# Folding an attention memory into gate weights: split float32 passes, or plain float32 tiles of 64 rows by 32 columns

## The chip, the cores and the metric

The kernel runs on one core of one Trainium2 chip. The metric is the device time of one execution in microseconds (us). Engines are called by the names of the profile: PE is TensorE's matmuls and PEld its weight loads, DVE is VectorE, ACT is ScalarE, POOL is GpSimd, SP is SyncE, which issues most DMAs.

## The reference

Attention to a memory of 32 slots for each of 8 heads and 4 batches, then a gated layer and a second layer for 2304 tokens (the softmax sums carry + 1e-9, left out here):

```python
a = softmax(phi, axis=2)                      # over the 576 tokens
k_m = einsum('bhsm,bhsd->bhmd', a, k)         # 32 x 64 for each head
v_m = einsum('bhsm,bhsd->bhmd', a, v)
attn = softmax(q @ k_m.T / 8) @ v_m           # 4 x 8 x 576 x 64
x = attn, tokens by 512
x = ((x @ w_a) * (x @ w_b)) @ w_o1            # 512 -> 1536 -> 512
h = x @ w_in                                  # 512 -> 2048
out = (h * sigmoid(1.702 h)) @ w_out          # 2048 -> 512
```

## The kernel before

The attention's last product is never made. Since `x @ w_a` is `P @ (v_m @ w_a)` with P the softmax weights of a batch (576 tokens by 8 heads x 32 slots), the kernel **folds** the memory into the weights: for each batch and each of six groups `g` of 256 hidden columns it makes `eff = v_m @ [w_a | w_b]`, 256 rows (in two chunks `c` of 4 heads) by 512 columns. `gated` multiplies P with eff, `proj` with w_o1.

PE multiplies float32 exactly enough in two ways. One is a plain float32 matmul, which the trace shows as two records. The other splits both operands into a high and a low part that fit a shorter format (`hi_lo`: ACT writes the high part, DVE or POOL subtracts it) and makes three ordinary passes, high x high, low x high, high x low (`PASSES`). Nearly all matmuls of the kernel are of the second kind.

The folds before:

- Group 0 (`fold0`, L756) runs in the attention phase, batch by batch, in plain float32. `bdv[b]` holds the memory of a batch as the stationary operand: 128 partitions are 2 heads of 64, and for each pair `r` of heads 64 columns are the 2 x 32 slots, zero where head and slot don't belong together. Two matmuls of 128 rows by 64 columns fill a bank.
- Groups 1 to 5 (`fold`, L787) run behind the attention for two batches `2 pb` and `2 pb + 1` together. `split_memory` has split bdv into `vhl`; `decode_piece` and `split_weights` have decoded each piece of w_a and w_b (128 rows, 256 columns of both) from the 64-bit input and split it too. For each pair of heads three passes of 128 x 128 with 512 values streamed fill one bank: the upper 64 partitions belong to one batch, the lower to the other. Most folds are in two halves of two pairs each, at different places of `main`.
- `fold_out` (L802, L804) takes a bank away: ACT writes the high part of eff, DVE the low one, before in two instructions each of 64 partitions.

Buffers: eight PSUM banks; `dm_s`, three to six temporary buffers in which inputs are decoded; `wab_s`, four places for split weights of the fold, inside the tile `wv`, which the trace names in L787. `close_attention` makes the tiles of the second phase when the attention is over.

The order on each engine is set when the program is built. Streams of steps (generators) ask for an engine, a time and a duration; `Order.run` keeps a clock for each engine and takes the step that can start first. On the chip each engine works through its list in that order and waits by semaphores for its operands. `Lengths.three` is the planner's guess for three passes. `main` is the stream that sets PE's order behind the attention.

Of the kernel before, what the change touches and what calls it, by code (L numbers as in the profile page):

```python
# [8 lines left out]
F32 = mybir.dt.float32  # L9
# [17 lines left out]
MBN = 8  # L27
HOLDD = {4: ("attn", 1, 0), 6: ("attn", 3, 0)}
# [6 lines left out]
PW0 = 4  # L35
PW = 5.5
# [138 lines left out]
def tile_mem_attention_moe_moe2(  # L175
# [195 lines left out]
    slots_of = {"wab": wab_s, "o1": whl_s}  # L371
    decoded = {}

    def decode(first, last, prio):
        if first in HOLDD:
            yield ("mark", *HOLDD[first])
        for i in range(first, last):
            name, part, _, n = pieces[i]
            t = yield "mark", "raw", i
            m = yield "slot", dm_s  # L380
# [23 lines left out]
    def decode_piece(t, i, name, part, n, m):  # L404
# [31 lines left out]
        if plain:  # L436
            dm_s.release(m, t)
            od.mark(t, *name, part)
        elif name[0] == "in":
# [14 lines left out]
        else:  # L454
# [4 lines left out]
            yield from split_weights(t, name, part, wt[name][0], m, dst, n)  # L459

    def w_ab_view(tile_):
        return tile_.rearrange("p (i r f) -> p i r f", i=2, r=1)
# [4 lines left out]
    def split_weights(t, name, part, whole, m, src, n):  # L467
        view = {"o1": w_out_view, "wab": w_ab_view}[name[0]](whole)
        r = slice(part * n, (part + 1) * n)
        t = yield from hi_lo(t, view[:, HI, r, :], view[:, LO, r, :], src, 512)  # L470
        dm_s.release(m, t)
        od.mark(t, *name, part)
# [8 lines left out]
    def row(b, h):  # L481

        return (h + 2 * (b % 2)) % HG * M
# [200 lines left out]
    def close_attention():  # L684
# [4 lines left out]
        for c in range(NHG):  # L689
            yield "mark", "eff", 0, B - 1, c, 0  # L690
# [6 lines left out]
        nonlocal py, pz  # L697
        py = tc.alloc_tile_pool(name="py", bufs=1, side="right", reuse_waits="tile")
        pz = tc.alloc_tile_pool(name="pz", bufs=1, side="right", reuse_waits="tile")
        n = 4 * CW  # L700
        big["y0"] = y0 = py.tile([P, 7 * 4 * N2 + 8], F32R, name="y0")
        nw = 2 * NHG * n
        big["wv"] = wv = pz.tile([P, nw + B // 2 * 2 * 2 * NHG * P], F32R, name="wv")
        wab_m, vhl_m = wv[:, :nw], wv[:, nw:]
# [3 lines left out]
        give(wab_s, [wab_m[:, i * n:(i + 1) * n] for i in range(2 * NHG)])  # L708
# [7 lines left out]
        for i in (HI, LO):  # L716
# [3 lines left out]
        vhl.extend(x.rearrange("p (i r m) -> p i r m", i=2, r=2 * NHG) for x in (  # L720
            vhl_m[:, i * 4 * NHG * P:(i + 1) * 4 * NHG * P] for i in range(B // 2)
        ))
        od.spawn(8, split_memory())


    py, pz, vhl, g1_t, g1_all, eff_y, big = None, None, [], {}, [], [], {}
# [21 lines left out]
    def fold0(b):  # L748
        for c in range(NHG):
# [4 lines left out]
            for r in range(2):  # L754
                o = row(b, 2 * r)
                nc.tensor.matmul(  # L756
                    ps[0][o:o + D, :], bdv[b][:, 2 * c + r, :], wt["wab", 0, 2 * c + r][0], start=True, stop=True
                )
            od.spawn(0, fold_out(t, 0, b, c, 0, slice(0, P), ps, [1]))

    def split_memory():

        for b in range(B):
            t = 0.0
            for c in range(NHG):
                t = max(t, (yield "mark", "bdv", b * NHG + c))
            for e in range(2):
                o = (e + b) % 2 * 2 * M
                dst = vhl[b // 2].rearrange("p i (c e) m -> p i c e m", e=2)[:, :, :, e, o:o + 2 * M]
                src = bdv[b].rearrange("p (c e) m -> p c e m", e=2)[:, :, e, :]  # L770
                t1 = yield from hi_lo(t, dst[:, HI], dst[:, LO], src, 2 * D)
                od.mark(t1, "vhl", b, e)
        more = [[bdv_m[:, i * 512:(i + 1) * 512], t1] for i in range(2)]
# [3 lines left out]
    def fold(g, pb, pairs=range(2 * NHG)):  # L777
        t0 = 0.0
        for b in (2 * pb, 2 * pb + 1):
            for e in range(2):  # L780
                t0 = max(t0, (yield "mark", "vhl", b, e))
        for r in pairs:
            t = max(t0, (yield "mark", "wab", g, r, 0))
            t, ps = yield PE, t, Lengths.three, bank_m
            w = w_ab_view(wt["wab", g, r][0])
            for n, (sw, mv) in enumerate(PASSES):
                nc.tensor.matmul(  # L787
                    ps[0], vhl[pb][:, sw, r, :], w[:, mv, 0, :], start=(n == 0), stop=(n == len(PASSES) - 1)
                )
            if pb == B // 2 - 1:  # L790
                wab_s.release(wt["wab", g, r], t)
            left = [2]
            for i in range(2):
                half = (i + r) % 2
                od.spawn(
                    i, fold_out(t, g, 2 * pb + i, r // 2, half, slice(half * D, (half + 1) * D), ps, left)
                )

    def fold_out(t, g, b, c, part, half, ps, left):
        hi, lo = (eff_of(g, b)[c][half, i, :] for i in (HI, LO))  # L800
        t, _ = yield ACT, t, act(512, True)
        nc.scalar.activation(out=hi, in_=ps[0][half, :], func=AF.Copy)  # L802
        t, _ = yield DVE, t, dve(512)
        nc.vector.tensor_tensor(out=lo, in0=ps[0][half, :], in1=f32(hi), op=ALU.subtract)  # L804
        left[0] -= 1
        if left[0] == 0:
            bank_m.release(ps, t)
        od.mark(t, "eff", g, b, c, part)

    def gated(g, b, u):  # L810
        t0 = 0.0
        for c in range(NHG):
            t0 = max(t0, (yield "mark", "attn", b * NHG + c, u))
            for i in range(2 if g else 1):
                t0 = max(t0, (yield "mark", "eff", g, b, c, i))
# [146 lines left out]
    def room_early():  # L962

        crowded()
        rest = views(big["y0"], YN, 9, 14 * WN)
# [142 lines left out]
    def combine_weights(g):  # L1108
        m = [decoded[("in", g), k] for k in range(2)]
        t = yield "mark", "decoded", ("in", g), 0  # L1110
        t = max(t, (yield "mark", "decoded", ("in", g), 1))
        s = yield "slot", win_s
# [321 lines left out]
    def main():  # L1434
# [14 lines left out]
        yield from fold(1, 1, range(NHG))  # L1449
# [140 lines left out]
```

## Time and profile before

| what | value |
|---|---|
| time, median of 3 runs | 782.17 us (781.64 to 783.31) |
| the profiled execution's own time | 783.01 us |
| its span | 781.2 us |
| PE busy | 768.4 us, 98% |
| DVE, ACT, POOL busy | 82%, 53%, 47% |
| chain that ended last | PE 92%, of it the gate L831 18%, the fold L787 3% |

The span is the time from the first to the last instruction of the program. The chain that ended last is followed back from the last instruction; shares of PE on it are read as what the end depends on. A matmul's record starts when PE takes it and its end is modelled, so a step's cost to PE is the distance of starts. Times on ACT, DVE and POOL matter where PE waits for them. In the groups by line, "64x512 fp32r" is what one instruction writes; a weight load or matmul has its rows and columns in the array ahead of that, as 128*64.

### The profile page before, as it was taken

Reading aid. Unit: us, or ns where it says so; the run is one execution under the profiler, and the core shown is the slowest. Engines: PE = TensorE matmul, PEld = TensorE weight load, DVE = VectorE, ACT = ScalarE, POOL = GpSimd, SP = SyncE. Lnnn points to the kernel's source line nnn. Section 1 sums busy time; section 2 is a strip of 40 time slices with the busy share of each in tenths; the row PEclk is TensorE's granted clock in tenths of the full one; section 3 lists DMA queues with packets and bytes.
Section 4 is the critical chain, followed back from the end, with each engine's and each line's share of the span. In section 5 each row is a group of like instructions: output and inputs, shape, how many; then the busy total and the mean of one; then the engine's idle time right before and its main releaser. Section 6 shows DMA issues by size and latency. Waiting matters only on the chain.

```text
span 781.2 us, 14295 instructions
## 1 busy us (share of the span) xinstructions
PE 768.4 (98%) x5216; PEld 708.7 (91%) x5216; DVE 638.7 (82%) x1132; ACT 416.9 (53%) x924; POOL 369.6 (47%) x347
## 2 busy tenths in 40 slices
PE   8999999999999999999999999999999999999997
PEld 7777789999989899899999999999998878889997
DVE  4878988999999987886989777777796786857886
ACT  4567768664655645544755555544563445534442
POOL 1223215554645544535799666333261036763563
PEclk9999999999999999999999999999999999999999
DMA  8856510122222312130013635544678855934421
GB/s 283 331 176 200 159 29 28 55 81 81 71 65 85 105 56 81 55 98 11 1 29 97 209 130 185 176 156 156 201 254 288 273 170 186 292 88 135 137 81 29
DMA packets 70183, 103.96 MB, mean 133 GB/s; under 512 B 5856, under 2 KB 48864, under 8 KB 70112
## 3 DMA queue, kind: packets, MB, share of 16 engines
q1 hardware_dynamic: 64656, 93.64, 37.7%
q10 hardware_dynamic: 5456, 9.41, 3.4%
q8 instruction: 41, 0.67, 0.4%
q14 instruction: 30, 0.25, 0.1%
HBM read 75.24 MB, written 27.79 MB: 132 GB/s over the span
## 4 chain that ended last, share of the span: by engine, by line
PE 92%; DVE 3%; DMA 2%; ACT 1%; issue 1%; POOL 1%; SPq 0%; ACTq 0%; DVEq 0%; POOLq 0%
PE bank L1135 22%; PE bank L831 18%; PE bank L1336 14%; PE bank L1367 10%; PE bank L864 10%; PE bank L887 10%; PE bank L787 3%; DMA phi<-in_phi_dram 1%; PE bank L619 1%; PE bank L575 1%; DMA kv<-in_v_dram 1%; PE bank L756 1%; PE bank L494 1%; ACT et L547 0%; DVE mx L541 0%
## 5 line engine op out<-in xcount | busy, mean ns | idle before, releaser
L1177 DVE TENSOR_TENSOR acc<-bank,acc 128x384 f32<-128x384 f32 x168 | 89.7, 553 | 31.6 <-PE bank L1135 19.5
L302 DVE TENSOR_TENSOR attn<-acc,attn 128x512 fp32r<-128x512 f32 (+2 forms) x94 | 90.7, 987 | 25.0 <-ACT attn L308 25.0
L302 POOL TENSOR_TENSOR acc<-acc 128x512 f32<-128x512 f32 (+2 forms) x63 | 81.0, 1299 | 46.1 <-DVE attn L302 24.2
L308 ACT ACTIVATE attn<-acc 128x512 fp32r<-128x512 f32 (+2 forms) x114 | 66.4, 602 | 55.0 <-PE bank L1367 18.0
L1187 ACT ACTIVATE acc<-acc 128x384 f32<-128x384 f32 x96 | 49.3, 523 | 52.7 <-DVE acc L1177 51.7
L844 ACT ACTIVATE gr<-bank 128x288 f32<-128x288 f32 x96 | 38.8, 404 | 65.2 <-PE bank L831 63.7
L302 POOL TENSOR_TENSOR y<-gr,y 128x288 fp32r<-128x288 f32 x40 | 36.3, 908 | 50.3 <-ACT y L308 50.2
L847 DVE TENSOR_TENSOR gr<-bank,gr 128x288 f32<-128x288 f32 x96 | 43.0, 450 | 14.4 <-PE bank L831 8.5
L831 PE MATMUL bank<-attn,eff 128*128 128x288 f32 x384 | 54.3, 296 | 0.0
L831 PEld LDWEIGHTS bank<-attn,eff 128*128 128x128 f32 x384 | 52.1, 188 | 1.3 <-issue 0.9
L864 PE MATMUL bank<-g,whl_b 128*128 128x288 f32 x384 | 52.8, 295 | 0.1
L1135 PE MATMUL bank<-attn,y 128*128 128x384 f32 x288 | 52.3, 335 | 0.0
L864 PEld LDWEIGHTS bank<-g,whl_b 128*128 128x128 f32 x384 | 51.7, 188 | 0.6 <-POOL whl_b L302 0.3
L887 PE MATMUL bank<-y,whl_a 128*128 128x512 f32 (+1 forms) x240 | 51.5, 370 | 0.0
L1135 PEld LDWEIGHTS bank<-attn,y 128*128 128x128 f32 x288 | 50.1, 188 | 0.0
L419 POOL TENSOR_SCALAR dm<-dm 128x512 f32<-128x512 f32 x21 | 34.6, 1651 | 32.1 <-ACT dm L417 32.1
L302 POOL TENSOR_TENSOR y<-acc,y 128x256 fp32r<-128x256 f32 (+1 forms) x22 | 20.1, 924 | 61.7 <-ACT y L308 61.7
L887 PEld LDWEIGHTS bank<-y,whl_a 128*128 128x128 f32 x240 | 41.9, 188 | 8.0
L302 POOL TENSOR_TENSOR g<-gr,g 128x288 fp32r<-128x288 f32 x28 | 27.0, 967 | 40.8 <-ACT g L308 40.6
L907 DVE TENSOR_TENSOR acc<-bank,acc 128x512 f32<-128x512 f32 (+1 forms) x72 | 38.4, 552 | 5.9 <-PE bank L887 5.2
L1336 PE MATMUL bank<-wv,attn 128*128 128x512 f32 x180 | 43.0, 393 | 0.0
L417 ACT ACTIVATE dm<-raw 128x512 f32<-128x512 f32 x41 | 27.0, 667 | 28.3 <-DMA raw<-in_moe_w_b_dram 12.3
(269 smaller groups left out, 2024.4 us busy)
## 6 DMA issues: line engine op xcount, KB each, us to landing
g2d<-acc SPq DMA_DIRECT2D x96, 192.0 KB, 2.3
raw<-in_moe_w_out_dram SPq DMA_DIRECT2D x28, 512.0 KB, 4.5
acc<-g2d SPq DMA_DIRECT2D x10, 1024.0 KB, 6.0
raw<-in_moe_w_in_dram SPq DMA_DIRECT2D x16, 512.0 KB, 3.8
acc<-g2d SPq DMA_DIRECT2D x16, 512.0 KB, 5.8
raw<-in_moe_w_a_dram SPq DMA_DIRECT2D x20, 256.0 KB, 2.7
raw<-in_moe_w_b_dram SPq DMA_DIRECT2D x20, 256.0 KB, 3.0
q<-in_q_dram SPq DMA_DIRECT2D x8, 576.0 KB, 6.3
```

The costliest lines, as they stand in the source:

```text
L302: (nc.gpsimd if e == POOL else nc.vector).tensor_tensor(out=dst, in0=in0, in1=in1, op=op)
L308: nc.scalar.activation(out=hi, in_=src, func=AF.Copy)
L831: nc.tensor.matmul(ps[0][:, :U], e[c][:, sw, i * CW + j * P:i * CW + (j + 1) * P], attn(b, mv, c, u * U, U), start=(n == 0), stop=(n == 3 ...
L844: nc.scalar.activation(out=gr[0], in_=pa_[0][:, :U], func=AF.Copy)
L847: nc.vector.tensor_tensor(out=gr[0], in0=pb[0][:, :U], in1=gr[0], op=ALU.mult)
L864: nc.tensor.matmul(ps[0][:, :U], w[:, sw, j, mb * P:(mb + 1) * P], g1[0][:, j, mv, :], start=(n == 0), stop=(n == 3 * G1 - 1),)
L887: nc.tensor.matmul(ps[0][:, :e - o], w[:, sw, j, mb * P:(mb + 1) * P], g1_all[mv][:, j, o:e], start=(n == 0), stop=(n == 3 * G1 - 1),)
L1135: nc.tensor.matmul(ps[0][:, :N2], w[:, sw, r, :], y[mv][r], start=(n == 0), stop=(n == 5))
L1177: nc.vector.tensor_tensor(out=s[0], in0=ps[0][:, :N2], in1=x[0], op=ALU.add)
L1187: nc.scalar.activation(out=c[0], in_=c[0], func=AF.Gelu_apprx_sigmoid)
L1336: nc.tensor.matmul(ps[i, s][0], b[0][:, sw, c - o, :], wo2[c][:, mv], start=(c == n == 0), stop=(c == 4 * K4 - 1 and n == 2),)
L1367: nc.tensor.matmul(ps[name][0][:, :NB], x[0][:, sw, c, :], moving(b, h // 2 + c, mv), start=(h == c == n == 0), stop=(h > 0 and c == K4 - ...
```

## The change

The fold of groups 1 to 5 uses plain float32 and no split operands. For a pair of batches it is made in one piece: 16 matmuls, each of 64 rows (one head's 64 values) by 32 columns (its 32 slots), with 512 values streamed, into four banks (one for each batch `i` and chunk `c`). `z` is the half of the 64-row tiles: 0 the upper partitions, 1 the lower. Eight matmuls, of both halves, four column places and two batches, stand one behind the other and use different parts of the array; the upper and the lower ones write different banks. The second eight fill what is missing.

With that the memory isn't split but copied (`bdw`, in the tile `plain`), the weights stay where they were decoded (ten buffers of `plain` from piece 10 on, for group 1 the four of `dm_s`), `fold_out` takes a whole bank of 128 partitions, and `fold0` uses four matmuls of 128 x 32, since `row` gives each head's place anew. Folds stand where one of their halves stood.

```diff
+ALONE = 10
+FOLD = 2000
...
-            m = yield "slot", dm_s
+            m = yield "slot", wab_s if i >= ALONE and name[0] in ("wab", "o1") else dm_s
...
+        elif name[0] == "wab":
+            wt[name] = m
+            od.mark(t, *name, part)
...
-        return (h + 2 * (b % 2)) % HG * M
+        return (h + b % 2) % HG * M
...
-        big["wv"] = wv = pz.tile([P, nw + B // 2 * 2 * 2 * NHG * P], F32R, name="wv")
-        give(wab_s, [wab_m[:, i * n:(i + 1) * n] for i in range(2 * NHG)])
+        pv = tc.alloc_tile_pool(name="pw", bufs=1, side="right", reuse_waits="tile")
+        plain = pv.tile([P, (NWB * 2 + 4) * CW], F32, name="plain")
+        give(wab_s, views(plain, nw, NWB))
...
-            for r in range(2):
-                o = row(b, 2 * r)
+            for h in range(HG):
+                r, k = divmod(h, 2)
                 nc.tensor.matmul(
-                    ps[0][o:o + D, :], bdv[b][:, 2 * c + r, :], wt["wab", 0, 2 * c + r][0], start=True, stop=True
+                    ps[0][row(b, h):row(b, h) + M, :], bdv[b][:, 2 * c + r, k * M:(k + 1) * M],
+                    wt["wab", 0, 2 * c + r][0], start=True, stop=True,
                 )
...
-            for e in range(2):
-                t1 = yield from hi_lo(t, dst[:, HI], dst[:, LO], src, 2 * D)
+            t, e = yield {POOL: pool(H * M), ACT: act(H * M)}, t
+            dst, src = (x[b].rearrange("p r m -> p (r m)") for x in (bdw, bdv))
...
-        for r in pairs:
-            t = max(t0, (yield "mark", "wab", g, r, 0))
-            t, ps = yield PE, t, Lengths.three, bank_m
-            for n, (sw, mv) in enumerate(PASSES):
-                nc.tensor.matmul(
-                    ps[0], vhl[pb][:, sw, r, :], w[:, mv, 0, :], start=(n == 0), stop=(n == len(PASSES) - 1)
-                )
+        ps = {}
+        for i in range(2):
+            for c in range(NHG):
+                t, ps[i, c] = yield PE, t - HOP_PE, FOLD if len(ps) == 3 else 0.0, bank_m
+        for k in range(NHG):
+            for z in (k, 1 - k):
+                c, rows_ = k if z == 0 else 1 - k, slice(z * D, (z + 1) * D)
+                for h in (z, z + 2):
+                    r = 2 * c + h // 2
+                    for i in range(2):
+                        b = 2 * pb + i
+                        o = row(b, h)
+                        nc.tensor.matmul(
+                            ps[i, c][0][o:o + M, :], bdw[b][rows_, r, z * M:(z + 1) * M],
+                            wt["wab", g, r][0][rows_, :], start=True, stop=True,
+                        )
...
-        nc.scalar.activation(out=hi, in_=ps[0][half, :], func=AF.Copy)
+        nc.scalar.activation(out=hi, in_=ps[0], func=AF.Copy)
...
-        yield from fold(1, 1, range(NHG))
+        yield from fold(1, 1)
...
-        yield from fold(2, 0, range(NHG))
...
-        yield from fold(2, 0, range(NHG, 2 * NHG))
+        yield from fold(2, 0)
...
-                if n % 2 == 0:
-                    nxt = (g, 1) if n < B else (g + 1, 0)
-                    h = n % B // 2
-                    yield from fold(*nxt, range(h * NHG, (h + 1) * NHG))
+                if n == 0:
+                    yield from fold(g, 1)
+                elif n == 6:
+                    yield from fold(g + 1, 0)
```

On PE, up to the first fold of group 1 only the fold of group 0 differs. PE at that first fold, before (a row is an instruction with the tiles that it writes and reads, its shape, and how many follow each other):

```order
L864 MATMUL bank_75<-g_95,whl_a 128x288 x6
L787 MATMUL bank_72<-wv 128x512 x3
L787 MATMUL bank_77<-wv 128x512 x3
L787 MATMUL bank_71<-wv 128x512 x3
L787 MATMUL bank_73<-wv 128x512 x3
L864 MATMUL bank_76<-g_95,whl_a 128x288 x6
```

Now, the first round of eight and the start of the second (L800 is the new fold, L873 the former L864; `dm` and `dm_x` are the four temporary buffers that hold the weights of group 1):

```order
L873 MATMUL bank_75<-g_95,whl_a 128x288 x6
L800 MATMUL bank_72<-dm_85,plain 32x512
L800 MATMUL bank_71<-dm_85,plain 32x512
L800 MATMUL bank_72<-dm_x_103,plain 32x512
L800 MATMUL bank_71<-dm_x_103,plain 32x512
L800 MATMUL bank_77<-dm_83,plain 32x512
L800 MATMUL bank_73<-dm_83,plain 32x512
L800 MATMUL bank_77<-dm_84,plain 32x512
L800 MATMUL bank_73<-dm_84,plain 32x512
L800 MATMUL bank_72<-dm_85,plain 32x512
L800 MATMUL bank_71<-dm_85,plain 32x512
```

Banks 72 and 71 are written by the upper half of the first round and the lower half of the second, 77 and 73 the other way round; all four are full only at the end.

DVE at the outputs of the same fold, before:

```order
L423 TENSOR_SCALAR dm_85<-dm_85 128x512
L427 SCALAR_TENSOR_TENSOR dm_85<-raw_80,dm_85 128x512
L804 TENSOR_TENSOR eff<-bank_72,eff 64x512
L804 TENSOR_TENSOR eff_b<-bank_72,eff_b 64x512
L804 TENSOR_TENSOR eff<-bank_77,eff 64x512
L804 TENSOR_TENSOR eff<-bank_71,eff 64x512
L804 TENSOR_TENSOR eff<-bank_73,eff 64x512
L804 TENSOR_TENSOR eff_b<-bank_77,eff_b 64x512
L804 TENSOR_TENSOR eff_b<-bank_71,eff_b 64x512
```

Now (L816 is the output; L422 to L435 are steps in which later weights are decoded from their raw form):

```order
L422 TENSOR_SCALAR plain<-plain 128x512
L426 TENSOR_SCALAR plain<-plain 128x512
L430 SCALAR_TENSOR_TENSOR plain<-raw_80,plain 128x512
L435 SCALAR_TENSOR_TENSOR plain<-raw_80,plain 128x512
L422 TENSOR_SCALAR plain<-plain 128x512
L426 TENSOR_SCALAR plain<-plain 128x512
L816 TENSOR_TENSOR eff<-bank_72,eff 128x512
L816 TENSOR_TENSOR eff<-bank_77,eff 128x512
L816 TENSOR_TENSOR eff_b<-bank_71,eff_b 128x512
L816 TENSOR_TENSOR eff_b<-bank_73,eff_b 128x512
```

Eight outputs of half a bank became four of a whole one, and six decode steps stand ahead of them instead of two.

## Rows read from the trace of the kernel before

**Rows 1.** The page: PE's busy time; granted clock in 40 slices.

```profile
PE 768.4 (98%) x5216; PEld 708.7 (91%) x5216; DVE 638.7 (82%) x1132; ACT 416.9 (53%) x924; POOL 369.6 (47%) x347
...
PEclk9999999999999999999999999999999999999999
```

**Rows 2.** Table by stage: stretch, length, busy us of PE, PEld, DVE, ACT, POOL; clock.

```profile
110.00:200.00 90.00, 89.92 (x646) 87.85 (x645) 81.84 (x152) 57.48 (x132) 44.55 (x41) 1.00 0.17 54
200.00:300.00 100.00, 100.00 (x592) 90.54 (x591) 93.97 (x159) 54.61 (x116) 51.63 (x44) 1.00 0.27 85
```

**Rows 3.** Time line of PE, 120 to 160 us: start, length, instructions merged.

```profile
126.01 2.90 PE L787 MATMUL bank<-wv 128*128 128x512 f32 x12
128.75 3.36 PE L864 MATMUL bank<-g,whl_a 128*128 128x288 f32 x24
131.95 3.33 PE L831 MATMUL bank<-attn,eff 128*128 128x288 f32 x24
135.11 1.55 PE L787 MATMUL bank<-wv 128*128 128x512 f32 x6
136.50 3.36 PE L831 MATMUL bank<-attn,eff 128*128 128x288 f32 x24
```

**Rows 4.** Groups by line on PE: count, busy us, mean ns, idle time before.

```profile
L787 PE MATMUL bank<-wv 128*128 128x512 f32 x120 | 30.6, 393 | 0.0
```

**Rows 5.** Time line of PE, 105.6 to 110.2 us: scores, gate, fold of group 0.

```profile
106.53 0.66 PE L831 MATMUL bank<-attn,eff_x 128*128 128x288 f32 x3
107.02 0.56 PE L831 MATMUL bank<-attn,eff_p 128*128 128x288 f32 x3
107.52 0.69 PE L619 MATMUL bank<-qT,bdk 128*32 128x288 f32 x8
108.14 1.94 PE L756 MATMUL bank<-wab,bdv 128*64 128x512 f32 x8
110.01 0.40 PE L864 MATMUL bank<-g,whl_a 128*128 128x288 f32 x1
```

**Rows 6.** Time line of the weight loads, 107 to 110.3 us.

```profile
107.51 0.16 PEld L619 LDWEIGHTS bank<-qT,bdk 128*32 128x32 f32 x8 [0.17 <-DVE sT L625]
108.14 0.20 PEld L756 LDWEIGHTS bank<-wab,bdv 128*64 128x64 f32 x4 [0.47 <-issue]
108.62 0.14 PEld L756 LDWEIGHTS bank<-wab,bdv 128*64 128x64 f32 x2 [0.29 <-issue]
109.05 0.14 PEld L756 LDWEIGHTS bank<-wab,bdv 128*64 128x64 f32 x2 [0.28 <-issue]
```

**Rows 7.** Groups by line on ACT and DVE: outputs of folds.

```profile
L802 ACT ACTIVATE eff<-bank 64x512 fp32r<-64x512 f32 x24 | 14.1, 590 | 2.5 <-PE bank L787 2.2
L802 ACT ACTIVATE eff<-bank 128x512 fp32r<-128x512 f32 x4 | 2.4, 595 | 0.9 <-PE bank L756 0.9
...
L804 DVE TENSOR_TENSOR eff<-bank,eff 64x512 fp32r<-64x512 f32 x24 | 16.5, 686 | 2.5 <-ACT eff L802 1.3 <-ACT eff_b L802 0.8
L804 DVE TENSOR_TENSOR eff<-bank,eff 128x512 fp32r<-128x512 f32 x4 | 2.7, 679 | 0.3 <-ACT eff L802 0.2
```

**Rows 8.** Groups by line on ACT and POOL: weights split into two parts.

```profile
L308 ACT ACTIVATE wv<-dm 128x512 fp32r<-128x512 f32 x11 | 6.7, 625 | 1.4 <-DVE dm L432 1.4
...
L302 POOL TENSOR_TENSOR wv<-dm,wv 128x512 fp32r<-128x512 f32 x12 | 15.8, 1325 | 23.8 <-ACT wv L448 12.6 <-ACT wv L308 6.2 <-DVE g L804 5.0
```

**Rows 9.** Time line of DVE, 124 to 140 us: two decode steps, first outputs.

```profile
126.59 0.78 DVE L423 TENSOR_SCALAR dm<-dm 128x512 uint32<-128x512 uint32 x1
127.41 0.69 DVE L427 SCALAR_TENSOR_TENSOR dm<-raw,dm 128x512 uint32<-128x512 uint32 x1
128.14 0.68 DVE L804 TENSOR_TENSOR eff<-bank,eff 64x512 fp32r<-64x512 f32 x1
```

**Rows 10.** Time line of DVE, 95 to 98.5 us: last decode step of group 1.

```profile
96.79 0.68 DVE L432 SCALAR_TENSOR_TENSOR dm<-raw,dm 128x512 uint32<-128x512 uint32 x1
```

## What the change will do to the time

> **What bounds the kernel now.** I read the page's busy times first, then the table by stage, then the groups and time lines of the step that is changed. TensorE (PE) is busy 98% of the span, at the full granted clock in every slice, 2.4 GHz of its two levels [rows 1]. The table shows where that holds: from 110 us on, PE is busy 89.92 of 90 us, then 100.00 of 100 [rows 2]. VectorE (DVE) has the next highest share, 91 and 94% in these two stretches, and yet PE has next to no idle time. So behind 110 us a microsecond taken from PE comes off the end, and one taken from another engine does not. The fold of groups 1 to 5 lies entirely in that part.
>
> What the fold costs PE is read from starts in its time line, since the modelled ends overlap the next start [rows 3]. A fold in one piece starts at 126.01 and the next step at 128.75: 2.74 us for twelve passes. Half a fold starts at 135.11 and what follows at 136.50: 1.39 us for six. There are 120 such passes without idle time before them [rows 4]; they come as two pieces of twelve and sixteen of six, so the ten folds hold PE 2 x 2.74 + 16 x 1.39 = 27.7 us.
>
> **What the change does, part by part.** *The new fold's time on PE.* Instead of 12 passes of 128 rows by 128 columns a fold has 16 plain float32 matmuls of 64 rows by 32 columns. What one costs, and whether several run together, is read from two float32 steps of the attention. The fold of group 0 (L756) has matmuls of 128 rows by 64 columns with 512 values streamed; each shows as two records. Eight of them, four matmuls, start at 108.14, and the next step at 110.01: 1.87 us [rows 5]. Their weight loads start at 108.14, 108.62 and 109.05 [rows 6], so one record takes 0.43 us, two tiles that lie side by side in the columns share this time, and the four steps are 4 x 0.43 plus 0.15 for the first load and the drain. The scores (L619) put four tiles of 32 columns side by side: eight records with 288 streamed start at 107.52 and are over at 108.14, 0.62 us [rows 5]. One after the other they would take eight times about 0.24 (0.43 x 288/512), 1.9 us; four at once and two records deep, 0.48 and a drain. So tiles of different columns run at once, at float32 too.
>
> Eight at once, 16 tiles are two rounds of two records: the four steps of L756, 1.87 us. Around it lie the costs of changing the tile shape. Three ordinary matmuls of 288 take 3 x 0.13 = 0.40 us in a run (24 of them from 131.95 to 135.11 [rows 3]), but 0.49 behind the scores and 0.50 ahead of them [rows 5]: 0.09 and 0.10. Loads of neighbouring tiles start 0.007 us apart (eight in 0.16 us, one being near 0.11 [rows 6]), so eight tiles add some 0.04 to the last start. Sum: 1.87 + 0.19 + 0.04 = 2.10 us, 21.0 for ten folds, **6.7 us less**.
>
> *What no row shows* is two tiles on the same columns and different rows at the same time; every step of the trace uses all 128 rows. The bounds are from L756: at best the lower half of the rows is as free as another column group (2.10 us a fold); at worst the two halves of the rows take turns, eight steps of 0.43 in place of four (3.82 us). I take the best end. The nearest rows, L619 and L756, show groups of the array with operands and weights of their own streaming at once for the whole length of a record, and within a round the order gives the two row halves different banks, so they do not share a place to write to. In between lies the case that the streams run together but the weight loads of the two halves do not: each of the four steps longer by a load of 0.11, 2.54 us a fold and 2.3 us gained in all.
>
> By the Trainium skill (TensorE: Matmul & The Clock Gate, Part 3, on packing small matmuls) tiles that differ in rows and columns run at once, sixteen of 32 by 32 in the time of one matmul and about 4 ns for each further tile. No run here shows it for float32; by it, as an estimate, the sum would be what I took.
>
> *The fold of group 0* goes from two tiles of 64 columns to four of 32, all side by side: the same number of steps in both rows above, so 0, within 0.3 us either way for its eight calls. It is the only thing that changes on PE ahead of 110 us.
>
> *Emptying the banks.* Before, a fold's results leave by eight ACT and eight DVE instructions on 64 partitions; the rows show 590 and 686 ns for them, and 595 and 679 for one on 128 partitions [rows 7]. Four do now what eight did: 40 x 0.59 us less on ACT, 40 x 0.69 on DVE. The splits of w_a and w_b into high and low parts go as well (ACT 625 ns, POOL 1325 or DVE for each of twenty pieces [rows 8]). None of it was on PE's path, so it is worth nothing at the end; it buys slack. Against it stands that four banks fill at the same moment. From the fold's end the first bank is free after 0.59 + 0.69 = 1.3 us, the last after about 0.6 + 4 x 0.69 = 3.4. PE meanwhile has four other banks: a group of four chains of six matmuls at 0.13, 3.1 us, or of 0.23, 5.4 us. The i-th chain behind that needs the i-th bank, so with DVE at hand there are 1.8 us of cover or more. Without it every fold costs what the outputs are late.
>
> *The weights.* A fold now needs all four pieces of its group at once, where half a fold needed two. Group 1 keeps four temporary buffers until its second fold; the ten new ones take the later groups. The last of the four pieces of group 1 is decoded at 97.5 us [rows 10] and folded at 126, so 28 us cover the first fold, and the later groups have more buffers than they had. The four copies of the memory on POOL replace splits on three engines. I cost this at 0; if the cover went, the first fold would be late by what is missing.
>
> *Whole folds for halves.* Of the folds for the first pair of batches the first half moves to where the second stood, of those for the second pair the second half to where the first stood. So no result is nearer to its use than the nearest was. The tightest place stays the first fold, which was in one piece before: the next gate starts at 131.95, 3.2 us behind its end at 128.75 [rows 3], and needs two of the four outputs, 0.59 + 2 x 0.69 = 2.0 us. Cost 0 as long as ACT and DVE come to them at once.
>
> **Rivals.** *The row halves take turns.* Then a fold is 8 x 0.43 + 0.15 + 0.23 = 3.82 us, ten are 38.2, and the kernel is 10.5 us **slower**, 792.7. It decides from the point where a fold takes over 2.77 us, that is, from six steps on. For it: no row shows otherwise. Against it: the independence of the column groups.
>
> *A column's two tiles queue.* The tile below on the same columns starts its first record only when the one above has started its second. With the order upper, lower, lower, upper that is six steps: 6 x 0.43 + 0.15 + 0.23 = 2.96 us a fold, 1.9 us slower, 784.1.
>
> *The gain comes but is eaten by waits.* DVE works in the written order, and at the first fold its four outputs stand behind six decode steps of later weights; such steps take 0.7 to 0.8 us each in the time line [rows 9]. One of them late for its data holds the outputs, and PE at the next gate. With 0.4 us at each fold 4 us are lost: 779.5. For it: DVE is at 94% in the second stretch [rows 2]. Against it: DVE loses 28 us of work there. The Trainium skill (TensorEngine Tiling (Array Packing), PSUM Bottleneck) warns of just this, that tiling speeds up TensorE but not the emptying of PSUM; before, the trace shows no PE idle time from it, and each bank's output is here half as long in instructions as it was.
>
> **How the numbers follow.** The profiled execution took 783.01 us (span 781.2), 0.84 above the median of 782.17. 783.01 - 6.7 = 776.3; against the median 775.5, which I predict. Chances: eight at once 0.70 (775 to 780 with the slower loads, most near 775.5); gain partly eaten 0.12 (778 to 782); a column's tiles queue 0.08 (784); the halves take turns 0.10 (793). The range for 8 in 10 goes from 774.3 (fold 0 and spread of the runs on the good side) to 782.0 and leaves out the last two. About 0.2%, 1.6 us, is what a measurement can tell from no change: faster holds the first case and most of the second, 0.79; same 0.07; slower 0.14.
>
> **What would show it.** Right: the starts of the new matmuls show two rounds, and from the first to the next ordinary matmul 1.9 us; eight weight loads within 0.1 us; PE busy without idle time from 110 us on; the front as before to a few tenths. Wrong: starts of the lower rows 0.4 or 0.9 us behind the upper ones, six or eight steps in a fold; idle time of PE ahead of the gate or projection behind a fold, released by DVE.

## The result, and the profile after

The changed kernel takes **773.33 us** (773.26 to 773.78) against 782.29 us (781.64 to 783.31) for the kernel before on the same chip: a ratio of 0.9885, with a 95% interval of 0.9868 to 0.9903. It is faster by 9.0 us; forecast were 6.7, and 773.33 lies 1.0 us below the low end of the range. In two further comparisons the gain was 8.1 us both times (below). So direction and mechanism came as forecast and the size did not.

The line numbers have moved: the fold is L800 (was L787), its outputs L814 and L816 (L802 and L804), the gate L840 (L831), the projection L873 (L864), the scores L622 (L619). The page of after, busy us of each engine (share of the span), answers to [rows 1]; the table by stage to [rows 2], with the same columns:

```profile
PE 760.2 (99%) x5448; PEld 691.2 (90%) x5448; DVE 602.4 (78%) x1084; ACT 382.7 (50%) x858; POOL 343.2 (44%) x329
...
PEclk9999999999999999999999999999999999999999
```

```profile
110.00:200.00 90.00, 90.00 (x736) 83.21 (x735) 78.68 (x153) 47.66 (x110) 38.53 (x36) 1.00 0.26 83
200.00:300.00 100.00, 100.00 (x696) 86.53 (x695) 83.06 (x149) 42.55 (x93) 40.25 (x38) 1.00 0.29 87
```

PE is still what sets the end: no idle time from 110 us on, the full clock in every slice. DVE fell from 94% to 83% of the second stretch.

The time line of PE at the first fold (start, length, operation, instructions merged) answers to [rows 3]; below it a later fold, where the weights have one name, so that its 32 records stand in one row:

```profile
121.59 3.36 PE L873 MATMUL bank<-g,whl_a 128*128 128x288 f32 x24
124.89 0.62 PE L800 MATMUL bank<-dm,plain 64*32 64x512 f32 x2
124.90 0.62 PE L800 MATMUL bank<-dm_x,plain 64*32 64x512 f32 x2
124.91 1.02 PE L800 MATMUL bank<-dm,plain 64*32 64x512 f32 x6
125.35 0.60 PE L800 MATMUL bank<-dm_x,plain 64*32 64x512 f32 x2
125.37 1.02 PE L800 MATMUL bank<-dm,plain 64*32 64x512 f32 x10
125.81 0.60 PE L800 MATMUL bank<-dm_x,plain 64*32 64x512 f32 x2
126.20 0.62 PE L800 MATMUL bank<-dm,plain 64*32 64x512 f32 x6
126.24 0.60 PE L800 MATMUL bank<-dm_x,plain 64*32 64x512 f32 x2
126.77 3.44 PE L873 MATMUL bank<-g,whl_a 128*128 128x288 f32 x24
130.04 3.32 PE L840 MATMUL bank<-attn,eff 128*128 128x288 f32 x24
```

```profile
167.21 1.95 PE L800 MATMUL bank<-plain 64*32 64x512 f32 x32
169.09 3.45 PE L873 MATMUL bank<-g,whl_b 128*128 128x288 f32 x24
```

The first eight records start within 0.05 us of each other, whether their rows are the upper or the lower ones; the next eight stand 0.45 us behind, then come two more steps of 0.43. From the first start to the next ordinary matmul are 1.88 us (124.89 to 126.77, 167.21 to 169.09; forecast 1.87). Eight tiles do run at once. With the dearer neighbours on both sides a fold costs 2.08 us, by its starts against the 0.13 us pitch of ordinary matmuls around it; the ten make 20.83, against 27.77 before by the same reading. That is **6.94 us** (forecast 6.7).

The fold of group 0 has changed too, though it was forecast at nothing. The first two rows are from before, where its first call meets the scores, the next two from after:

```profile
19.30 1.08 PE L756 MATMUL bank<-wab,bdv 128*64 128x512 f32 x4
20.31 0.69 PE L619 MATMUL bank<-qT,bdk 128*32 128x288 f32 x8
```

```profile
18.65 1.07 PE L756 MATMUL bank<-wab,bdv 128*32 128x512 f32 x8
19.53 0.67 PE L622 MATMUL bank<-qT,bdk 128*32 128x288 f32 x8
```

From this fold to the scores 1.01 us became 0.88. With tiles of 32 columns on both sides of the border the array keeps its shape, and the change of shape between 128 x 64 and 128 x 32 is gone. Two more visits that are followed by tiles of 32 columns lost the same 0.13 us, and the last visit, whose predecessor is a score, 0.11 at its start and 0.04 inside; the three visits between tiles of 128 columns lost 0.01 or 0.02. Over the whole attention phase this step fell from 10.13 to 9.55 us with its borders: **0.57 us**.

The outputs, minimum, median and maximum in ns, answer to [rows 7]; below them DVE at the first fold:

```profile
L814 ACT ACTIVATE eff<-bank x16: 580/594/600, 58.2 to 366.8; 128x512 fp32r<-128x512 f32 x16
```

```profile
L816 DVE TENSOR_TENSOR eff<-bank,eff x16: 653/682/692, 59.0 to 367.6; 128x512 fp32r<-128x512 f32 x16
```

```profile
127.96 0.43 DVE L422 TENSOR_SCALAR plain<-plain 128x512 f32<-128x512 f32 x1 [0.72 <-ACT plain L420]
128.43 0.43 DVE L426 TENSOR_SCALAR plain<-plain 128x512 uint32<-128x512 uint32 x1
128.77 1.28 DVE L816 TENSOR_TENSOR eff<-bank,eff 128x512 fp32r<-128x512 f32 x2
```

They last as long as forecast, but come later. The fold ends at 126.77; DVE first finishes decode steps that wait for ACT, and its first output starts only at 128.77 and ends at 129.45. The gate that needs it starts at 130.04. Of the 1.8 us or more of cover that the prediction counted 0.6 are left. The second output that this gate needs ends at 130.05, half a microsecond ahead of the gate's fifth matmul, which needs it (as the stops with half outputs show, below). The cover holds, by little.

### The profile page after: what moved, and what is told of

It reads as the page before. It is cut to its first block, busy times and chain, and to the rows that moved or that the text cites. A ratio compares the mean times of both kernels' runs of the same rounds, so it can differ in the third digit from the quotient of the medians.

```text
span 771.5 us, 14636 instructions
## 1 busy us (share of the span) xinstructions
PE 760.2 (99%) x5448; PEld 691.2 (90%) x5448; DVE 602.4 (78%) x1084; ACT 382.7 (50%) x858; POOL 343.2 (44%) x329
## 4 chain that ended last, share of the span: by engine, by line
PE 93%; DVE 3%; DMA 2%; ACT 1%; issue 1%; SPq 0%; ACTq 0%; DVEq 0%
PE bank L1148 23%; PE bank L840 19%; PE bank L1349 14%; PE bank L1380 10%; PE bank L873 10%; PE bank L896 10%; PE bank L800 2%; DMA phi<-in_phi_dram 1%; PE bank L622 1%; PE bank L578 1%; DMA kv<-in_v_dram 1%; PE bank L497 1%; PE bank L756 1%; ACT et L550 0%; DVE mx L544 0%
## 5 line engine op out<-in xcount | busy, mean ns | idle before, releaser
L840 PE MATMUL bank<-attn,eff 128*128 128x288 f32 x384 | 54.6, 297 | 0.0
L840 PEld LDWEIGHTS bank<-attn,eff 128*128 128x128 f32 x384 | 52.0, 188 | 2.9 <-issue 0.9
L873 PEld LDWEIGHTS bank<-g,whl_b 128*128 128x128 f32 x384 | 51.4, 188 | 1.7 <-ACT g L310 1.7
L873 PE MATMUL bank<-g,whl_b 128*128 128x288 f32 x384 | 52.7, 296 | 0.0
L1349 PEld LDWEIGHTS bank<-wv,attn 128*128 128x128 f32 x180 | 33.9, 188 | 7.6
L840 PE MATMUL bank<-attn,eff_b 128*128 128x288 f32 x288 | 40.0, 295 | 0.0
L422 POOL TENSOR_SCALAR plain<-plain 128x512 f32<-128x512 f32 x15 | 24.5, 1636 | 34.3 <-ACT plain L420 34.3
```

The source lines that it names most:

```text
L840: nc.tensor.matmul(ps[0][:, :U], e[c][:, sw, i * CW + j * P:i * CW + (j + 1) * P], attn(b, mv, c, u * U, U), start=(n == 0), stop=(n == 3 ...
L873: nc.tensor.matmul(ps[0][:, :U], w[:, sw, j, mb * P:(mb + 1) * P], g1[0][:, j, mv, :], start=(n == 0), stop=(n == 3 * G1 - 1),)
L1349: nc.tensor.matmul(ps[i, s][0], b[0][:, sw, c - o, :], wo2[c][:, mv], start=(c == n == 0), stop=(c == 4 * K4 - 1 and n == 2),)
```

## The experiments

### The same two kernels again

The changed kernel in two further comparisons, and the kernel before in one more profiled execution, to part what belongs to the kernels from what one execution brings.

> The changed kernel once more, as it is. My account of the result: ten folds hold PE 20.8 us in place of 27.8 (6.9 us less), the fold of group 0 gains 0.6, a wait of 0.4 us at the split of w_out near 637 us is gone, and about 1 us of the 9.0 lies where the first inputs land and the last outputs leave, which differs from execution to execution. By it 773.3 us within 0.3, and the first step that waits for k and v (the softmax's first transposes) starts anywhere from 10.8 to 11.6 us. Rival: these ends were made shorter by the change itself; then the start is 10.8 again and the time behind the last matmul is 3.7 us again, against 4.4 before.

> The changed kernel once more, beside the next variant on the same chip. 773.3 to 774.1, as in its two looks so far.

> The kernel before, unchanged, for one more profiled execution: it tells which differences between the two traces belong to the kernels and which to one execution. The time of the kernel before so far is 781.64 to 783.31. In its first profile PE waited 0.43 us at 636.7 us (L1336, for the split of the memory), from the start of the last group of matmuls to the end of the span were 5.15 us, and the first transposes of the softmax started at 11.51 us. Theory A: the tail belongs to the order of the kernel before; then the tail is 5.0 to 5.2 again (kernels with the changed fold have 4.42 to 4.47). Theory B: the tail is a chance of one execution; then it may be 4.4 to 4.5. The wait at 636.7 was absent in the kernel with the first fold alone, which has the same order there: I expect 0 here, and 0.4 again if it belongs to the order. The first transposes: anywhere between 10.8 and 11.8.

The changed kernel took 774.02 us (773.39 to 775.47) against 782.14, a ratio of 0.9899 (0.9886 to 0.9913), and 773.84 (773.38 to 774.02) against 781.95, 0.9893 (0.9879 to 0.9906): 8.12 and 8.11 us. The first comparison shows 0.9 more, within the intervals. The first of these runs missed its expectation of 773.3 within 0.3. The kernel before took 782.97 us in its one more execution.

Four things differ between the first two profiles that are not the fold. The time line of PE late in the kernel, first before, then the same kernel once more:

```profile
636.70 0.42 PE L1336 MATMUL bank<-eff_b,attn 128*128 128x512 f32 x1
637.34 0.72 PE L1336 MATMUL bank<-eff_b,attn 128*128 128x512 f32 x2 [0.22 <-DVE eff_b L302]
```

```profile
637.01 0.85 PE L1336 MATMUL bank<-eff_b,attn 128*128 128x512 f32 x3
```

A pause of 0.4 us in the first is absent in the second: chance. (The second loses 0.5 around 172 us instead, and both spans are 781.2.) The first transposes of the softmax, behind the first transfers, started at 11.51 us in the first profile and at 11.32 in the second; with the changed kernel at 10.85, 11.74 and 10.99. Chance again, 0.9 us of it; it is nearly the whole difference between the spans of the changed kernel's first two profiles (771.5 and 772.4).

The third stays, and it is small. In the kernel before, a projection waits at 145 us for weights that POOL still has to split. The row is from the time line of the weight loads:

```profile
145.05 0.43 PEld L864 LDWEIGHTS bank<-g,whl_b 128*128 128x128 f32 x3 [0.32 <-POOL whl_b L302]
```

The matmul behind it starts **0.24 us** late. The second profile shows the same wait, and so does the kernel with the first fold alone (below); the changed kernel shows none there.

The fourth stays too. The stores that ACT issues at the end, in the time line of its queue, in the kernel before once more and in after; the last matmuls begin 1.0 us ahead of them in both:

```profile
776.81 1.47 ACTq L1419 DMA_DIRECT2D out_dram<-acc  x3
```

```profile
767.86 1.31 ACTq L1432 DMA_DIRECT2D out_dram<-acc  x3
```

From the start of the last matmul to the end of the span are 5.15 and 5.14 us in the two profiles of the kernel before, and 4.42 in the first two of the changed one. All eight profiles with the new folds have 4.4 to 4.5 there. So some **0.7 us** come with the new folds, in a part of the kernel that the change doesn't touch. The other stores leave and land alike; ACT's third is issued 1.92 us behind the start of the last matmul and lands at 4.1 in the kernel before, and is issued at 1.64 and lands at 3.4 in the changed one. The view of the DMA queues from 776 us on in the kernel before has a line that the last 4.5 us of the changed one don't have:

```profile
q14 instruction: 1, 0.01, 0.4%
```

This is one packet of 8 KB of instructions. It starts 2.6 to 3.0 us behind the start of the last matmul in all three profiles with the old folds; in the eight with the new ones the last such packet lies 5 us or more ahead of it. Whether it holds the store up wasn't tried, so the cause stays open.

### The first fold alone

The kernel before, with only the fold of group 0 in tiles of 32 columns:

```diff
-            for r in range(2):
-                o = row(b, 2 * r)
+            for h in range(HG):
+                r, k = divmod(h, 2)
                 nc.tensor.matmul(
-                    ps[0][o:o + D, :], bdv[b][:, 2 * c + r, :], wt["wab", 0, 2 * c + r][0], start=True, stop=True
+                    ps[0][row(b, h):row(b, h) + M, :], bdv[b][:, 2 * c + r, k * M:(k + 1) * M],
+                    wt["wab", 0, 2 * c + r][0], start=True, stop=True,
```

> The kernel before with one part of the change alone: the fold of group 0 in four tiles of 128 rows by 32 columns in place of two of 128 by 64; all else as before. If what this part gains is that its neighbours on PE (scores and memory sums of the attention, tiles of 32 columns too) need no change of the tile shape, its five places beside such steps take 0.88 us in place of 1.01 and the kernel is 0.4 to 0.6 us faster, 781.7 to 781.9. If, as I predicted, the part is worth 0, 782.3.

781.67 us (781.18 to 782.55) against 782.14; the ratio of 0.9994 has an interval of 0.9986 to 1.0003, so by time alone it is not told from nothing. The trace tells it:

```profile
18.93 1.06 PE L756 MATMUL bank<-wab,bdv 128*32 128x512 f32 x8
19.82 0.67 PE L619 MATMUL bank<-qT,bdk 128*32 128x288 f32 x8
```

0.89 us as in after, and 9.55 in all. The gain of this part doesn't need the rest of the change. Its end has 5.01 us, nearly that of before, and the packet of instructions lies there too, so the shorter end belongs to the rest of the change.

### No row halves

The new fold with matmuls of all 128 rows: 16 for a fold as before, each with zeros at the other head's rows, so only four tiles, of different columns, can share the array.

```diff
-                            ps[i, c][0][o:o + M, :], bdw[b][rows_, r, z * M:(z + 1) * M],
-                            wt["wab", g, r][0][rows_, :], start=True, stop=True,
+                            ps[i, c][0][o:o + M, :], bdw[b][:, r, z * M:(z + 1) * M],
+                            wt["wab", g, r][0], start=True, stop=True,
```

> The changed kernel with each of the 16 matmuls of a fold on all 128 rows (the memory has zeros at the other head's rows, so the result is the same): four tiles side by side, none below another. Four rounds of two records of 0.43 us in place of two rounds: 8 x 0.43 + 0.15 + 0.23 = 3.8 us a fold, 17 us more than the changed kernel for ten, 790 to 791; slower than the kernel before. It would show that the rows' halves carry the gain. Rival: tiles below each other share what limits them, and the changed kernel's 2.08 us come from elsewhere; then the time is near 773.

790.8 us, in one run. The time line has the steps:

```profile
125.44 0.62 PE L800 MATMUL bank<-dm,plain 128*32 128x512 f32 x2
...
125.90 0.60 PE L800 MATMUL bank<-dm,plain 128*32 128x512 f32 x2
...
126.33 1.04 PE L800 MATMUL bank<-dm,plain 128*32 128x512 f32 x8
...
129.01 3.43 PE L873 MATMUL bank<-g,whl_a 128*128 128x288 f32 x24
```

3.57 us from the first start to the next ordinary matmul, eight steps instead of four, and 3.77 a fold with its borders. That is the price that the prediction's first rival named (3.82), reached by taking the row halves away. It is 17 us over the changed kernel: without the row halves plain float32 loses to the split passes.

### Outputs in halves

The prediction held that fewer instructions on ACT and DVE are worth nothing at the end. Two kernels have the new fold, but empty each bank of groups 1 to 5 in two halves of 64 partitions, as before. In the first the two halves of a bank follow each other:

```diff
-        t, _ = yield ACT, t, act(512, True)
-        nc.scalar.activation(out=hi, in_=ps[0], func=AF.Copy)
-        t, _ = yield DVE, t, dve(512)
-        nc.vector.tensor_tensor(out=lo, in0=ps[0], in1=f32(hi), op=ALU.subtract)
+        for half in ([slice(0, P)] if g == 0 else [slice(0, D), slice(D, P)]):
+            t1, _ = yield ACT, t, act(512, True)
+            nc.scalar.activation(out=hi[half], in_=ps[0][half, :], func=AF.Copy)
+            t2, _ = yield DVE, t1, dve(512)
+            nc.vector.tensor_tensor(out=lo[half], in0=ps[0][half, :], in1=f32(hi[half]), op=ALU.subtract)
+        t = t2
```

> The changed kernel with the outputs of the folds of groups 1 to 5 again in two halves of 64 partitions, eight instructions on ACT and eight on DVE for each fold in place of four and four: 24 us more on ACT, 27 us more on DVE. If the gain is PE's alone, this work lies beside PE and the time stays at 773.3 within 0.4. If the 2 us beyond the forecast came from the relief of DVE and ACT, it is 775 or more.

I missed by 10 us: 783.29 (782.77 to 784.5) against 782.14, ratio 1.0015 (1.0006 to 1.0024). The whole gain is gone, although the folds still cost 2.08 us. The time line of PE and of DVE behind the first fold, and PE behind the second:

```profile
127.15 3.43 PE L875 MATMUL bank<-g,whl_a 128*128 128x288 f32 x24
131.32 0.91 PE L842 MATMUL bank<-attn,eff 128*128 128x288 f32 x4 [0.74 <-DVE eff L817]
132.56 2.90 PE L842 MATMUL bank<-attn,eff 128*128 128x288 f32 x20 [0.33 <-DVE eff L817]
...
142.20 3.46 PE L842 MATMUL bank<-attn,eff_b 128*128 128x288 f32 x24 [1.17 <-DVE y L817]
```

```profile
129.24 2.03 DVE L817 TENSOR_TENSOR eff<-bank,eff 64x512 fp32r<-64x512 f32 x3
131.81 0.69 DVE L817 TENSOR_TENSOR eff<-bank,eff 64x512 fp32r<-64x512 f32 x1 [0.54 <-ACT eff L815]
```

The gate stops twice. It goes on at 131.32, when the third half is out (129.24 + 2.03 = 131.27), and at 132.56, when the fourth is (131.81 + 0.69 = 132.50). In after the two whole outputs that this gate needs are over at 130.05. Such stops stand behind most folds. Set against after, instruction by instruction, PE falls 9.3 us behind between 110 and 500 us, which is the whole loss: ten stops of 0.3 to 1.3 us make 6.9 of it, the rest are steps of 0.1 to 0.3 beside them.

The second kernel lets the two halves of a bank go as streams of their own, in case the order of the first was to blame. In `fold`, in place of the one output stream:

```diff
-                od.spawn(0, fold_out(t, g, 2 * pb + i, c, ps[i, c]))
+                left = [2]
+                for e in range(2):
+                    od.spawn(e, fold_half(t, g, 2 * pb + i, c, slice(e * D, (e + 1) * D), ps[i, c], left))
```

> The changed kernel with half outputs again, but the two halves of a bank as two independent streams, as the kernel before has them. In the earlier variant a bank's second half was planned behind its first, 2.6 us for a bank in a row. If the 9 us lost there were that chain, this is back near 773.3, within 1 us. If the number of instructions on DVE is the cause (eight times 0.69 = 5.5 us behind each fold against 3.1 us of cover), the loss stays: 778 to 784, with PE idle ahead of gates and projections behind the folds.

783.22 (782.42 to 784.6) against 781.95, ratio 1.0016 (1.0007 to 1.0025). The loss is the same in both orders of the halves. It looks different, though: fewer and longer stops, and something behind them. PE at the first gate (in brackets the idle time before and what ended it), then rows of the table by stage, whose third number from the end is the granted clock:

```profile
132.05 0.40 PE L853 MATMUL bank<-attn,eff 128*128 128x288 f32 x1 [1.75 <-ACT eff L825]
132.96 4.65 PE L853 MATMUL bank<-attn,eff 128*128 128x288 f32 x23 [0.52 <-DVE eff L827]
```

```profile
134.00:136.00 2.00, 2.00 (x11) 2.00 (x10) 1.42 (x3) 0.58 (x2) 1.49 (x1) 0.51 0.00 0
136.00:137.00 1.00, 1.00 (x9) 1.00 (x9) 0.89 (x3) 0.43 (x2) 0.00 (x0) 1.00 0.30 68
```

```profile
178.00:180.00 2.00, 0.86 (x6) 0.62 (x5) 2.00 (x4) 1.98 (x5) 0.00 (x0) 1.00 0.00 0
...
181.00:183.00 2.00, 2.00 (x10) 2.00 (x10) 1.43 (x4) 0.92 (x2) 1.00 (x1) 0.50 0.00 0
```

After the two stops, 1.9 and 0.8 us against after, the granted clock is 0.51, the lower of its two levels of 1.2 and 2.4 GHz, and 23 matmuls last 4.65 us, where 24 last 3.32 in after (at 130.04). After the stops of 1.2 and 1.8 us around 178 it is 0.50. Each time some 1.5 us more are lost, 3.0 of the 10 us by which this profile falls behind that of after. In the kernel with chained halves the clock stays at 1.00.

### Two folds joined

If a change of tile shape costs something at both ends of a fold, two folds in a row should save one pair of borders. The second fold of a group was put next to the first of the following group, four times; `joined_late` below leaves group 1 as it is.

```diff
-        yield from fold(1, 1)
         yield from gated(1, 0, 1)
...
         yield from gated(1, 1, 1)
+        yield from fold(1, 1)
+        yield from fold(2, 0)
...
-        yield from fold(2, 0)
...
-                if n == 0:
+                if n == 3:
                     yield from fold(g, 1)
-                elif n == 6:
                     yield from fold(g + 1, 0)
-                if late:
+                if late and n != 2:
```

> The changed kernel with the fold of the second pair of batches and the next group's fold for the first pair one behind the other on PE, four times (two of the ten folds stay alone). A fold costs 0.09 to change the tile shape, 0.05 for the first weight load, 0.10 for the drain and 0.11 for the first ordinary load behind it, 0.35 in all, which two joined folds pay once: 4 x 0.35 = 1.4 us less, 771.9. Rival: eight banks filled one after the other are not empty when the next steps need them, and PE waits: 773.3 or more.

774.04 (773.88 to 775.59) against 782.14, ratio 0.9901 (0.9888 to 0.9915): no better than the changed kernel next to it. In the later groups a pair costs 3.80 us instead of 2 x 2.08, as hoped. Behind the pair of group 1, PE waits:

```profile
147.95 1.92 PE L800 MATMUL bank<-plain 64*32 64x512 f32 x32
151.79 4.58 PE L873 MATMUL bank<-g,whl_b 128*128 128x288 f32 x21 [1.92 <-DVE y L816]
```

```profile
148.52 1.29 DVE L304 TENSOR_TENSOR whl_a<-plain,whl_a 128x512 fp32r<-128x512 f32 x1
149.73 0.68 DVE L430 SCALAR_TENSOR_TENSOR plain<-raw,plain 128x512 uint32<-128x512 uint32 x1
150.44 0.69 DVE L435 SCALAR_TENSOR_TENSOR plain<-raw,plain 128x512 uint32<-128x512 uint32 x1
151.06 2.48 DVE L816 TENSOR_TENSOR y<-bank,y 128x512 fp32r<-128x512 f32 x4
```

The pair fills all eight banks, and the first output stands on DVE behind the split and the decode of other weights. It ends at about 151.74 (151.06 + 0.68), and PE goes on at 151.79. This is the mechanism of the prediction's third rival, in a place where the cover is gone. Behind this wait, too, the granted clock falls to 0.50 (the table by stage from 154 us on):

```profile
154.00:156.00 2.00, 2.00 (x10) 2.00 (x10) 2.00 (x5) 0.68 (x1) 1.97 (x3) 0.50 0.03 9
```

The profiled execution is the slowest of this kernel, 775.59 at a mean clock of 0.998; the other three show 1.000 and 773.88 to 774.05, so the fall is probably not in each of them.

> The changed kernel with joined folds in groups 2 to 4 alone; group 1 keeps its two folds apart. Where all four were joined, the three later pairs held PE 3.80 us each in place of 2 x 2.08, and the first pair was followed by a wait of 2.0 us for the outputs of the folds. If these two numbers are all there is, this gives 3 x 0.36 = 1.1 us and loses nothing: 1.1 below the changed kernel of the same chip, about 772.6. Rival: the later places wait too once the early wait no longer holds PE back; then no difference.

772.64 (772.46 to 772.77) against 781.95, ratio 0.9878 (0.9863 to 0.9893), and 1.2 us under the changed kernel on the same chip (773.84). A pair in its time line, 3.60 us from its start to the next ordinary matmul, and no wait:

```profile
198.39 3.66 PE L800 MATMUL bank<-plain 64*32 64x512 f32 x64
201.99 5.77 PE L896 MATMUL bank<-y,whl_a 128*128 128x512 f32 x24
```

Three pairs save 3 x 0.36 = 1.1 us. It is the fastest kernel here.

## Why the prediction was wrong

**The bound** was read rightly. PE has no idle time behind 110 us, and microseconds taken from it came off the end one for one.

**The fold** came as forecast, 2.08 us for 2.10. The open question, two tiles on the same columns and different rows, is settled by the starts in the time line and by the kernel without row halves (3.77 us a fold). Of the rivals, "the row halves take turns" and "a column's two tiles queue" are out: lower rows start with the upper ones, and four steps are four. By the Trainium skill (TensorE: Matmul & The Clock Gate, Part 3) packed tiles run at once and each adds about 4 ns; the trace agrees that they run at once, for float32 too, but its starts are some 7 ns apart. The gain was 6.94 for 6.7: the folds before cost 0.07 more than counted, the new ones 0.17 less.

**The failed step is the fold of group 0**, "0, within 0.3 us either way". It gave 0.57. The steps inside were counted rightly, the borders not at all: I priced a change of tile shape around the new folds (0.09 and 0.10 from [rows 5]) and forgot that this fold stands beside the scores and the sums of the memory, whose tiles have 32 columns. [rows 5] had what was needed: the two stand next to each other, in different shapes. Where tiles of 32 columns follow, 0.13 us fall away (1.01 to 0.88). The Trainium skill (TensorEngine Tiling (Array Packing), Key Properties) says that a change of tiling mode drains TensorE; it gives no price, and these 0.13 us agree with the rule.

**A term is missing: the end of the kernel**, 0.7 us. The prediction didn't look there, and nothing in the diff points there. It is measured in all profiles and its cause is open.

**A small one was put at nothing: the relief of the side engines.** The prediction held the work that goes from ACT, DVE and POOL worth nothing at the end. In the kernel before, PE did wait once, at 145 us, for a split of w_o1 on POOL (it is why [rows 2] has 89.92 of 90 us), and that cost 0.24. It is gone with the change; whether by POOL's lighter load or by the moved folds wasn't tried.

Together 6.94 + 0.57 + 0.7 + 0.24 = 8.45 us. In the two further comparisons the medians of the spans differ by 8.45 and 8.55, those of the times by 8.1; a time holds 1.7 to 3.1 us beside its span. The two profiles of the first comparison are 9.7 us apart in span: beyond the 8.45 the start gave 0.66 and the pause 0.4, both chance, and 0.2 stay unassigned. **The range** had its low end only 1.2 us under the forecast, for group 0 and the spread; four terms that all fell on the good side by 0.2 to 0.7 us went through it.

**Emptying the banks**, "worth nothing at the end, it buys slack": right for the kernel before, and misleading for the one after. In this order of steps whole-bank outputs are a condition of the gain; half outputs with the decode steps behind them on DVE weren't tried. With half outputs the kernel is slower than before by 0.15%. The prediction counted the cover (1.8 us or more) "with DVE at hand", and DVE was not: 0.6 us were left. The third rival, a gain eaten by waits, did not happen, but it was nearer than its 0.12 reads. The rule that the prediction quoted beside it, of the Trainium skill (TensorEngine Tiling (Array Packing), PSUM Bottleneck), is that tiling speeds up TensorE but not the emptying of PSUM. The runs agree: with half outputs the same fast folds lost 783.29 - 774.02 = 9.3 us.

**The weights and the moved folds** cost nothing, as forecast; none of PE's waits in after is for either.

## What to carry to other kernels

- Small float32 products that need only 64 rows and 32 columns run eight at once, in the time that four of 128 rows take (a step of 0.43 us in both); without the row halves the same products lost to three split passes. Count the steps of the array, then the borders: a visit to another tile shape cost some 0.35 us here, so put visits of one shape side by side, also small steps that the change seems not to concern.
- A step that fills several banks in 2 us needs its outputs soon after. An output of 64 partitions costs ACT and DVE as much as one of 128, so whole banks halve that work; then look at what stands ahead of the first output on DVE in its written order. Both decide whether PE stops: with the same steps ahead it stopped for half outputs, and with whole outputs it stopped behind the joined pair of group 1.
- Where one profile of each kernel is compared, take a second of both before explaining half a microsecond.

## What the runs showed of the hardware

- Plain float32 with 512 values: each of the two records of a matmul takes a step of 0.43 us, whether two tiles of 128 x 64 share the array ([rows 6]), four of 128 x 32 or eight of 64 x 32; the second record of the first tile starts behind the first records of all eight.
- The starts don't keep to the written order of the tiles. In the second eight of a fold the code has the lower rows first, with the two matmuls on `dm_x` as third and fourth; in the trace they come last in both steps of that round (125.81 and 126.24).
- Stops of PE in a busy stretch were followed by the lower level of the granted clock (0.50 and 0.51) for some 3 us, which cost some 1.5 us more each time: 1.75 and 0.52 us of idle time around one matmul, 1.04 and 1.69 around six others, and 1.92 in one piece in the kernel with four joined pairs. So a late step on DVE or ACT can cost PE well over its own wait.
